# Attention and a rational FFN on one core: units chunk by chunk, four banks of sums, the reciprocal in SBUF

## The chip, the cores and the metric

The kernel runs on one core of one Trainium2 chip. Its time is device microseconds of one execution, the median of three runs. Engines: PE is TensorE (PEld its weight loads), DVE is VectorE, ACT is ScalarE, POOL is GpSimd, SP issues the DMAs. SBUF is the on-chip memory of the engines, PSUM the eight banks (128 x 512 fp32 each) into which PE writes.

## The reference

Two attentions in a row with 32 learned keys (`p`) for each head, and then a feed-forward layer whose activation is a rational function.

```python
def sm_attn(qq, kk, vv):
    s = scale * np.matmul(qq, kk.transpose(0, 1, 3, 2))
    a = np.exp(s - np.max(s, axis=-1, keepdims=True))
    a = a / (np.sum(a, axis=-1, keepdims=True) + 1e-09)
    return np.matmul(a, vv)
p_packed = sm_attn(p, k, v)              # 8 batches, 8 heads, 576 tokens, 64 wide
x = sm_attn(q, p_packed, p_packed)       # to (4608, 512)
h = x @ w_in                             # 512 x 2048
P = a[0] + a[1] * h + a[2] * h**2 + a[3] * h**3
Q = 1.0 + np.abs(b[0]) * np.abs(h) + np.abs(b[1]) * h**2
out = (P / (Q + 1e-6)) @ w_out           # 2048 x 512
```

The weights w_in and w_out come as float64; the kernel gets their 64-bit words.

## The kernel before

**Work and units.** There are 8 batches of 576 tokens. A batch's tokens are cut in two halves (x = 0, 1) of 288, and the 2048 columns between the two weight matrices in 8 chunks (c) of 256. One half of a batch with one chunk is a *unit*: 128 units in all, 16 for each batch (`units`, line 888). The second attention's product with w_in is folded: `m_chunk` (line 786) multiplies the packed values by one or two chunks of w_in into m, and `hidden` (line 814) multiplies m by the attention weights AH (and their low parts AL).

**A unit** goes through `hidden` in three steps. PE makes two tiles h (two banks in PSUM). ScalarE reads each three times (Y, U, sq), and VectorE makes the numerator Y from Y and h: a TENSOR_TENSOR and a SCALAR_TENSOR_TENSOR for each half; these four are called the front instructions here. GpSimd adds U and sq. Then ScalarE takes V = exp(-ln(U + 1)), and VectorE does three instructions with V, called the V instructions here: Y<-Y,abS,V, then V<-U,V, then Y<-V,Y (one Newton step of the reciprocal). V has a single buffer, in two banks of PSUM (`V_ring`, line 332). At the end Y is divided into a high and a low fp32r part: ScalarE casts gh, GpSimd subtracts gl, and GpSimd copies the last 32 of the half's columns to G.

**Sums.** `acc_block` (line 893) adds a unit's product with w_out to two banks of PSUM, three units later (LAG): three fp32r products (high x high, high x low, low x high) for each of two halves and two banks. The first 12 units (PLAIN) use one fp32 sum instead, with the undivided g and w_out (shown in the trace as two records each); their w_out is divided by `divide` (line 411) at units 11 to 21. Units run half by half, so two banks of sums are enough (`acc_ring`, line 330). `remainder` (line 865) handles the last 64 tokens of every batch, kept in G, for two batches at a time.

**Weights.** `load_words` (line 378) brings the 64-bit words of 16 chunks (8 of w_in, 8 of w_out) into free buffers (m, w), and `convert` (line 429) makes fp32 of them: two ScalarE passes of 1024 columns, and three VectorE instructions: a mask of the sign (TENSOR_SCALAR), a shift-and-or (SCALAR_TENSOR_TENSOR), an integer add of 1024 words (shown as CUSTOM_DVE_ANT_0 in the trace, as ISA in the order).

**Order.** All instructions are recorded and put in order by a `Planner` (line 25): it lists them by a table of costs, ways from engine to engine and DMA times, forward and back for four rounds, and writes each engine's instructions out in the planned order. Loads of the first batch stand first, in the order written (`pin`, line 212). Attention of batch b + 1 runs beside batch b's units, in 16 steps. Where the plan has PE idle in the first 150 us, `idle` (line 992) puts in products with a zero matrix. Nearly every instruction is issued in line 226, so rows are told apart by their tiles.

Of the kernel before, what the change touches and what calls it, by code (L numbers as in the profile page):

```python
# [31 lines left out]
class Planner:  # L32
# [7 lines left out]
    COST = {"vector": (70, 1.04), "scalar": (93, 0.83), "gpsimd": (215, 2.11), "tensor": (15, 0.417)}  # L40
    TRANSPOSE, F32 = (15, 0.834), (30, 1.667)
    WAY = {("vector", "vector"): 127, ("scalar", "scalar"): 143, ("tensor", "tensor"): 0, ("gpsimd", "gpsimd"): 0}
    WAY.update({(f"sync", x): 0 for x in ENGINES})
    PASS = 200
    ROUNDS = 4
    DMA_ISSUE, DMA_DELAY = 600, 2300
# [29 lines left out]
    def cost(self, engine, name, args, kwargs):  # L76
# [7 lines left out]
        if engine == "scalar":  # L84
            fixed += (aps[-1].space == PSUM) * -42 + ("accum_out" in kwargs) * 186 + ("bias" in kwargs) * 93
# [18 lines left out]
    def price(self, engine, calls):  # L104
        if engine != "tensor":
            return sum(self.cost(engine, *x) for x in calls)

        parts = {}
        for name, args, kwargs in calls:
            part = args[1].offset // args[1].ap[0][0], args[0].offset // args[0].ap[0][0]  # L110
            parts[part] = parts.get(part, 0) + self.cost(engine, name, args, kwargs)
        return max(parts.values()) + 7 * (len(calls) - 1)
# [36 lines left out]
    def schedule(self, before, after, rank, back=None):  # L149
# [6 lines left out]
        free = dict.fromkeys(self.ENGINES, 0.0)  # L156
# [3 lines left out]
        now = dma = 0.0  # L160
        left = n
        while left:
            for e in self.ENGINES:
                while soon[e] and soon[e][0][0] <= now:
                    heapq.heappush(ready[e], heapq.heappop(soon[e])[1:])
                if free[e] > now or not ready[e]:
                    continue
                _, i = heapq.heappop(ready[e])
                left -= 1
                start[i] = now  # L170
                end[i] = free[e] = now + self.costs[i]
                if e == "sync":
                    dma = max(dma, end[i]) + self.transfers[i]
                    end[i] = dma + self.DMA_DELAY
                for j in after[i]:
                    need[j] -= 1
                    f = self.ops[j][0]
                    way = self.WAY.get((e, f) if back is None else (f, e), self.PASS)
# [10 lines left out]
    def order(self):  # L189
        n = len(self.ops)  # L190
        self.costs = [self.price(*x) for x in self.ops]
        self.transfers = [self.transfer(calls[0][1]) if engine == "sync" else 0 for engine, calls in self.ops]
        before = self.edges()
# [6 lines left out]
        for r in range(self.ROUNDS):  # L200
# [4 lines left out]
            m = max(end)  # L205
# [52 lines left out]
def attention_rational_ffn(  # L258
# [31 lines left out]
    PLAIN = 12  # L290
    UNDIVIDED = {0: (0, 1), 4: (4, 5), 5: (6, 7)}
    DIVIDE = dict(zip((11, 12, 14, 15, 17, 18, 20, 21), (4, 5, 6, 7, 0, 1, 2, 3)))
    DIVIDED = {4: 1, 5: 2, 6: 3, 7: 4, 0: 5, 1: (2, 3), 2: 0, 3: (0, 4)}
    PRE = 4
    AHEAD = 5
    SCALE = 1.0 / float(D) ** 0.5
# [10 lines left out]
    zero = sb.tile([P, D], F32R, name="zero")  # L307
    win = sb.tile([P, NCH, NCC, CF], F32, name="win")
    G = sb.tile([P, NFC, 2 * REM], F32, name="G")
    cuts = [0, 2 * P, 4 * P, 4 * P + 3 * 2 * NB, 4 * P + 3 * 2 * NB + 30]  # L310
    small = sb.tile([P, cuts[-1]], F32, name="small")

    w_ring = Ring(sb, "w", NCH - 2, [P, 2, 2, DM], F32R)

    half_ring = Ring(sb, "half", 5, [P, 2, DM])
# [20 lines left out]
    def constants():  # L336
        nc.vector.tensor_scalar(zero, ident[:, 0:D], 0.0, None, ALU.mult)
# [30 lines left out]
    due = lambda x: x[1] // 2 + (LAG if x[0] == "out" else -2)  # L368
# [3 lines left out]
    room = [((m_ring, i), index["in", 4 * i] + 1) for i in range(NCH // 2)]  # L372
    room += [((w_ring, i), len(words)) for i in (1, 2, 3)]
    room += [((w_ring, i), index["out", 2 * UNDIVIDED[i][0]]) for i in (4, 5)]
    started = False
    words_in, converted = [], 0

    def load_words(n):
        while len(words_in) < min(len(words), converted + n):
            r = len(words_in)  # L380
            kind, i, n2 = words[r]
            used = [x for x, _ in words_in]
            free = [x for x, end in room if r < end and x not in used[converted:]]
            free = [x for x in free if x[0] is not w_ring or x[1] not in (2, 3) or started]
            if not free:
                return
            x = min(free, key=lambda x: max((j for j in range(r) if used[j] == x), default=-1))
            raw = x[0].at(x[1], [P, n2 * 512], I64)
# [8 lines left out]
            words_in.append((x, raw))  # L397

    W, X = {}, {}

    def undivided(c):
        if c not in X:
            pair = [i for i in UNDIVIDED if c in UNDIVIDED[i]]
            if pair:
                t = w_ring.at(pair[0], dtype=F32)
                X.update({y: t[:, x] for x, y in enumerate(UNDIVIDED[pair[0]])})
            else:
                X[c] = half_ring.at(c - 2)
        return X[c]

    def divide(c):
        place = DIVIDED[c]
        if isinstance(place, int):
            t = w_ring.at(place)
            hi, lo = W[c] = t[:, 0], t[:, 1]
        else:
            hi, lo = W[c] = [half_ring.at(i, dtype=F32R) for i in place]
        nc.scalar.copy(hi, X[c])
        for f in range(2):
            nc.gpsimd.tensor_sub(lo[:, f], X[c][:, f], hi[:, f].bitcast(F32))  # L420

    def o_next(dtype=None):
        return half_ring.at(1 if 3 in W else 4, dtype=dtype)
# [5 lines left out]
    def convert():  # L429
# [4 lines left out]
        (kind, i, n), raw = words[converted], words_in[converted][1]  # L434
# [4 lines left out]
        if kind == "in":  # L439
            dst = win[:, i // 2]  # L440
            di = dst.bitcast(I32)
        else:
            dst = undivided(i // 2)
# [597 lines left out]
```

## Time and profile before

| | us |
|---|---|
| median of 3 runs (786.75 to 788.15) | 787.98 |
| span of the profiled execution, first to last instruction | 786.0 |
| TensorE clock granted, mean | 0.987 |
| waits of ScalarE's sq on PE's h, in total | 31.0 |
| waits of VectorE's Y on ScalarE's V, in total | 23.0 |
| waits of PE on the first DMA of K | 15.2 |

The profile's page gives each engine's busy time, its busy share in 40 slices, the chain of work that ended last, and groups of equal instructions. A group's row has the line, the engine, the operation, the tiles written and read (buffer numbers left out), the shape, the count, then the busy time in us and the mean of one in ns, then the engine's idle time just before and what ended it. A row of the timeline has the start and the length in us, the engine, the operation and, in brackets, the idle time before it. A row of the chain has start, length and what it was. A busy PE is not necessarily PE at its peak.

### The profile page before, as it was taken

The numbers are of one execution on the slowest core, as the hardware profiler recorded it, in microseconds if no ns is written. First come the engines' busy times: TensorE is split into PE (matmuls) and PEld (weight loads), VectorE is DVE, ScalarE is ACT, GpSimd is POOL, SyncE is SP. The second block draws the span as 40 slices with busy tenths as digits, with TensorE's granted clock in tenths as the row PEclk, the third lists the DMA queues.
The fourth block names the chain that finished last, engine by engine and source line by source line (L and its number), as shares of the span: only waits on it lengthen the run. The fifth ranks groups of instructions, "written<-read, shape, count | busy, mean of one in ns | idle before, by whom it ended". The sixth has DMA issues, their size and how long they took to land.

```text
span 786.0 us, 14945 instructions
## 1 busy us (share of the span) xinstructions
PE 745.8 (95%) x5336; PEld 567.5 (72%) x5336; DVE 693.2 (88%) x1295; ACT 657.8 (84%) x1464; POOL 453.6 (58%) x448
## 2 busy tenths in 40 slices
PE   2679999999999999999999999999999999999997
PEld 1345555588778887678778887678787887778886
DVE  4899999998999789998999789998999789988873
ACT  5869978988896998888897898889798788998872
POOL 0012448757585665756686555756587556766663
PEclk9959999999999999999999999999999999999999
DMA  9984353023601155023601136023701132000001
GB/s 297 332 296 143 108 100 49 1 85 46 110 1 55 45 66 90 1 85 46 95 17 55 44 52 104 1 58 62 94 28 54 41 45 46 1 22 7 27 1 41
DMA packets 152027, 56.03 MB, mean 71 GB/s; under 512 B 122256, under 2 KB 141200, under 8 KB 151952
## 3 DMA queue, kind: packets, MB, share of 16 engines
q1 hardware_dynamic: 151952, 55.07, 30.7%
q8 instruction: 42, 0.69, 0.4%
q14 instruction: 33, 0.27, 0.1%
HBM read 45.62 MB, written 9.44 MB: 70 GB/s over the span
## 4 chain that ended last, share of the span: by engine, by line
PE 76%; ACT 10%; DVE 8%; DMA 4%; issue 1%; POOL 0%; SPq 0%; DVEq 0%; ACTq 0%
PE acc L226 38%; PE h L226 24%; PE at L226 14%; DVE Y L226 4%; ACT Y L226 2%; DMA nat<-in_k_dram 2%; DVE w L226 2%; ACT V L226 1%; ACT U L226 1%; ACT sq L226 1%; ACT kx L226 1%; ACT w L226 1%; DMA m<-in_moe_w_in_dram 1%; ACT m L226 1%; DVE small L226 1%
## 5 line engine op out<-in xcount | busy, mean ns | idle before, releaser
L226 POOL TENSOR_TENSOR U<-U,sq 128x576 f32<-128x576 f32 x128 | 184.1, 1438 | 109.1 <-ACT U L226 55.8
L226 PE MATMUL acc<-w,gh 128*128 128x512 f32 x736 | 239.3, 408 | 1.6 <-ACT gh L226 1.4
L226 PE MATMUL h<-AH,m 128*128 128x288 f32 x1024 | 201.1, 320 | 7.9 <-DVE Y L226 5.6
L226 PEld LDWEIGHTS h<-AH,m 128*128 128x128 f32 x1024 | 163.0, 191 | 45.8 <-DVE Y L226 22.6
L226 POOL TENSOR_TENSOR gl<-Y,gh 128x512 fp32r<-128x512 f32 x116 | 150.2, 1295 | 39.0 <-issue 14.3
L226 PEld LDWEIGHTS acc<-w,gh 128*128 128x128 f32 x736 | 131.8, 188 | 45.5 <-issue 11.8
L226 PE MATMUL acc<-w,gl 128*128 128x512 f32 x384 | 147.9, 412 | 0.0
L226 ACT ACTIVATE Y<-h,abS 128x288 f32<-128x288 f32 x256 | 126.3, 511 | 23.2 <-PE h L226 19.7
L226 ACT ACTIVATE sq<-h 128x288 f32<-128x288 f32 x256 | 107.0, 419 | 39.2 <-PE h L226 31.0
L226 DVE TENSOR_TENSOR Y<-Y,h 128x288 f32<-128x288 f32 x256 | 109.1, 444 | 26.3 <-ACT Y L226 9.7
L226 DVE SCALAR_TENSOR_TENSOR Y<-Y,abS,h 128x288 f32<-128x288 f32 x256 | 124.5, 504 | 2.2
L226 DVE SCALAR_TENSOR_TENSOR Y<-Y,abS,V 128x576 f32<-128x576 f32 x128 | 102.8, 803 | 23.6 <-ACT V L226 23.0
L226 ACT ACTIVATE U<-h 128x288 f32<-128x288 f32 x256 | 98.6, 424 | 9.8 <-PE h L226 4.7
L226 ACT ACTIVATE V<-U,one 128x576 f32<-128x576 f32 x128 | 98.4, 769 | 5.6 <-DVE Y L226 3.8
L226 PE MATMUL h<-AL,m 128*128 128x288 f32 x448 | 96.1, 295 | 0.0
L226 DVE SCALAR_TENSOR_TENSOR V<-U,V 128x576 f32<-128x576 f32 x128 | 96.0, 750 | 0.0
L226 PEld LDWEIGHTS acc<-w,gl 128*128 128x128 f32 x384 | 71.9, 188 | 23.9 <-issue 9.6
L226 DVE SCALAR_TENSOR_TENSOR Y<-V,Y 128x576 f32<-128x576 f32 x116 | 86.7, 748 | 1.9
L226 POOL COPY G<-Y 128x64 f32<-128x64 f32 x116 | 27.5, 237 | 102.6 <-DVE Y L226 95.6
L226 ACT ACTIVATE V<-V 128x576 f32<-128x576 f32 x128 | 84.8, 663 | 0.7
L226 PE MATMUL acc<-half,gh 128*128 128x512 f32 x240 | 78.4, 413 | 1.3 <-ACT gh L226 0.9
L226 ACT CAST gh<-Y 128x512 fp32r<-128x512 f32 x116 | 73.4, 632 | 6.0 <-DVE Y L226 5.5
(135 smaller groups left out, 984.1 us busy)
## 6 DMA issues: line engine op xcount, KB each, us to landing
w<-in_moe_w_out_dram SPq DMA_DIRECT2D x16, 512.0 KB, 4.6
out_dram<-half SPq DMA_DIRECT2D x15, 512.0 KB, 3.1
nat<-in_k_dram SPq DMA_DIRECT2D x48, 144.0 KB, 3.9
nat<-in_q_dram SPq DMA_DIRECT2D x48, 144.0 KB, 4.3
nat<-in_v_dram SPq DMA_DIRECT2D x24, 256.0 KB, 3.7
m<-in_moe_w_in_dram SPq DMA_DIRECT2D x8, 512.0 KB, 6.2
w<-in_moe_w_in_dram SPq DMA_DIRECT2D x8, 512.0 KB, 8.2
nat<-in_k_dram SPq DMA_DIRECT2D x4, 512.0 KB, 7.7
```

Of the source, the lines that this page charges most:

```text
L226: getattr(getattr(self.nc, engine), name)(*args, **kwargs)
```

## The change

- `units` runs chunk by chunk, both halves in turn; `acc_ring` has four banks, and `V_ring` is in SBUF, so that PSUM holds four banks of sums, two of h and two of the rest.
- PLAIN, `undivided` and `divide` are gone. A w_out chunk is divided as it is converted (ScalarE casts the high part, GpSimd subtracts the low one in two instructions), and every unit uses three fp32r products.
- The sign mask of `convert` is a GpSimd TENSOR_SCALAR in place of the VectorE one.
- Buffers for the words and for whole w_out chunks are two lists (RAW, WHOLE); chunks are due at twice the distance.
- The first loads are in another order, m_chunk, remainder and conversions stand at other units, and the transposed last keys go into kx by two copies in place of one into small.
- The planner has other costs and ways, a start time for each engine, a rule for GpSimd and some VectorE instructions that share a port (`shares`: TENSOR_SCALAR, copies and the integer add on SBUF alone), a limit of DMAs in flight, slack in the backward pass and eight rounds.

```diff
-    COST = {"vector": (70, 1.04), "scalar": (93, 0.83), "gpsimd": (215, 2.11), "tensor": (15, 0.417)}
+    COST = {"vector": (70, 1.04), "scalar": (93, 0.83), "gpsimd": (150, 2.14), "tensor": (15, 0.418)}
...
+    def shares(self, engine, calls):
+
+        if engine == "gpsimd":
+            return True
+        if engine != "vector":
+            return False
+        name, args, _ = calls[0]
+        aps = [x for x in args if isinstance(x, bass.AP)]
+        if any(x.space == PSUM for x in aps):
+            return False
+        return name in ("tensor_scalar", "tensor_copy") or (name == "tensor_add" and aps[0].dtype == I32)
...
-    PLAIN = 12
-    UNDIVIDED = {0: (0, 1), 4: (4, 5), 5: (6, 7)}
...
+    RAW = "m0 m1 m2 m3 w1 w2 w3 w4 m2 m3 w6 w7 w5 m0 m3 m0".split()
+    WHOLE = "o0 w5 o0 o0 m1 w6 o0 m1".split()
...
-    acc_ring = Ring(ps, "acc", 2, [P, DM])
+    V_ring = Ring(sb, "V", 1, [P, 2, HALF])
+    acc_ring = Ring(ps, "acc", 4, [P, DM])
     h_ring = Ring(ps, "h", 2, [P, 512])
-    V_ring = Ring(ps, "V", 1, [P, 2, 512])
     at_ring = Ring(ps, "at", 2, [P, 512])
...
-    due = lambda x: x[1] // 2 + (LAG if x[0] == "out" else -2)
+    due = lambda x: x[1] + (LAG if x[0] == "out" else -2)
...
-        nc.vector.tensor_scalar(lo, hi, -0x80000000, None, ALU.bitwise_and)
+        nc.gpsimd.tensor_scalar(lo, hi.bitcast(F32), 0.0, -2.0**31, ALU.is_lt, ALU.mult)
         nc.vector.scalar_tensor_tensor(hi, hi, 3, lo, ALU.logical_shift_left, ALU.bitwise_or)
-        nc.vector.tensor_add(dst.bitcast(I32), hi, di)
+        nc.vector.tensor_add(di, hi, di)
+        if kind == "out":
+            t = w_ring.at(i // 2)
+            wh, wl = W[i // 2] = t[:, 0], t[:, 1]
+            nc.scalar.copy(wh, dst)
+            for f in range(2):
+                nc.gpsimd.tensor_sub(wl[:, f], dst[:, f], wh[:, f].bitcast(F32))
...
-    units = [(bb, x, c) for bb in range(B) for x in range(2) for c in range(NCH)]
+    units = [(bb, x, c) for bb in range(B) for c in range(NCH) for x in range(2)]
...
-        if u < PLAIN:
-            for f in range(2):
-                g = GS[bb, x, c][:, f, cols]
-                nc.tensor.matmul(acc, g, X[c][:, f, :], start=c == 0 and f == 0, stop=c == NCH - 1 and f == 1)
...
-    for what in (2, "r", 3, "p", "k0", "k1", "qr", 4, "rv", "v0", "v1", 5, "q0", "q1"):
+    for what in ("r", "p", "qr", "k0", "k1", 1, "rv", "v0", "v1", 2, "q0", "q1", 3, 4):
```

How it moves instructions is shown at three places. First the DMA issues of SP at the program's start, before (AH is the buffer of the last keys there, pn of p, nat of K, m, w of words or of V and Q):

```order
L226 DMA m_1_75<-in_moe_w_in_dram 128x2x256 x2
L226 DMA m_2_76<-in_moe_w_in_dram 128x2x256 x2
L226 DMA AH_1_77<-in_k_dram 64x8x64
L226 DMA m_3_78<-in_moe_w_in_dram 128x2x256 x2
L226 DMA pn_1_79<-in_p_dram 32x2x64 x4
L226 DMA nat_1_80<-in_k_dram 128x4x256
L226 DMA nat_2_81<-in_k_dram 128x4x256
```

And the same place of SP after the change:

```order
L288 DMA AH_1_75<-in_k_dram 64x8x64
L288 DMA pn_1_76<-in_p_dram 32x2x64 x4
L288 DMA AH_1_75<-in_q_dram 32x4x128 x2
L288 DMA nat_1_77<-in_k_dram 128x4x256
L288 DMA nat_2_78<-in_k_dram 128x4x256
L288 DMA m_1_79<-in_moe_w_in_dram 128x2x256 x2
```

K (nat) is now ahead of all words of the weights; three loads of words stood ahead of it.

Second GpSimd from the first unit on, before (U is the denominator, half and w are w_out):

```order
L226 TENSOR_TENSOR U0_1_125<-U0_1_125,sq0_1_128 128x576
L226 TENSOR_TENSOR U1_2_137<-U1_2_137,sq0_2_140 128x576
L226 TENSOR_TENSOR U0_3_151<-U0_3_151,sq0_3_154 128x576
L226 TENSOR_TENSOR U1_4_166<-U1_4_166,sq0_4_169 128x576
L226 COPY pn0_3_241<-pn0_3_241 128x2x64
L226 TENSOR_TENSOR U0_5_180<-U0_5_180,sq0_5_183 128x576
L226 TENSOR_TENSOR half3_6_350<-w0_10_161,half2_5_349 128x512 x2
```

GpSimd at the same place after the change (TENSOR_SCALAR of 1024 columns is the mask):

```order
L288 TENSOR_TENSOR U0_1_127<-U0_1_127,sq0_1_130 128x576
L288 TENSOR_SCALAR w4_6_120<-w4_6_120 128x1024
L288 TENSOR_TENSOR w1_9_143<-w5_8_142,w1_9_143 128x512
L288 TENSOR_TENSOR U1_2_134<-U1_2_134,sq0_2_137 128x576
L288 COPY G_73<-Y0_1_129 128x2x32
L288 TENSOR_TENSOR w1_9_143<-w5_8_142,w1_9_143 128x512
L288 TENSOR_TENSOR gl0_1_160<-Y0_1_129,gh0_1_159 128x512
L288 TENSOR_TENSOR U0_3_150<-U0_3_150,sq0_3_153 128x576
```

Between two U of successive units there now stand masks, low parts of w_out, copies to G and gl.

Third PE at the first unit's sums (acc0 and acc1 are its two banks), before:

```order
L226 MATMUL acc0_13_171<-w0_10_161,gh0_1_160 128x512 x2
L226 MATMUL h0_7_170<-AH0_3_113,m1_6_134 128x288 x2
L226 MATMUL h1_8_175<-AH0_3_113,m1_6_134 128x288 x2
L226 MATMUL at1_28_178<-win_72,ppT0_1_88 32x256
L226 MATMUL at0_29_179<-win_72,ppT0_1_88 32x256
```

PE at that place after the change:

```order
L288 MATMUL acc0_13_169<-w0_7_122,gh0_1_159 128x512 x2
L288 MATMUL acc1_14_170<-w0_7_122,gh0_1_159 128x512 x2
L285 MATMUL acc1_14_170<-w0_7_122,zero_71 32x256 x2
L288 MATMUL h0_7_168<-AH0_3_112,m0_6_124 128x288 x2
L288 MATMUL acc0_13_169<-w0_7_122,gl0_1_160 128x512
L288 MATMUL acc0_13_169<-w0_7_122,gh0_1_159 128x512 x2
L288 MATMUL acc1_14_170<-w0_7_122,gl0_1_160 128x512
L288 MATMUL acc1_14_170<-w0_7_122,gh0_1_159 128x512 x2
```

The two fp32 sums of a bank became six products, with gl among them, so that PE's sums now need GpSimd's gl; zero products stand where the plan has PE idle (12 in the first program, 55 now).

More of the change, by code (lines that the diff above doesn't have):

```diff
@@ L84, in cost @@
         if engine == "scalar":
-            fixed += (aps[-1].space == PSUM) * -42 + ("accum_out" in kwargs) * 186 + ("bias" in kwargs) * 93
+            fixed += (aps[-1].space == PSUM) * -42 + ("accum_out" in kwargs) * 93 + ("bias" in kwargs) * 93
+            per += 0.1 * any(x.ap[-1][0] == 2 for x in aps[:2])
+        if engine == "gpsimd" and len(aps) < 3:
+            fixed, per = 135, 0.9
         if engine == "vector" and len(aps) > 2 and any(self.columns(x) == 1 for x in aps[1:]):
@@ L147, in edges, with schedule @@
         return edges
-    def schedule(self, before, after, rank, back=None):
+    def schedule(self, before, after, rank, back=False):
         n = len(rank)
@@ L381, in load_words @@
             kind, i, n2 = words[r]
[L382 to L385, printed above, removed]
+            if RAW[r] in RAW[converted:r]:
                 return
-            x = min(free, key=lambda x: max((j for j in range(r) if used[j] == x), default=-1))
-            raw = x[0].at(x[1], [P, n2 * 512], I64)
+            raw = place(RAW[r], [P, n2 * 512], I64)
             if kind == "in":
@@ L396, in load_words @@
                     nc.sync.dma_start(raw[:, 512 * y : 512 * (y + 1)], w_out[(i + y) * P : (i + y + 1) * P, :])
[L397 to L418, printed above, removed]
-        for f in range(2):
-            nc.gpsimd.tensor_sub(lo[:, f], X[c][:, f], hi[:, f].bitcast(F32))
-    def o_next(dtype=None):
-        return half_ring.at(1 if 3 in W else 4, dtype=dtype)
+            words_in.append(raw)
+    W = {}
     def split(x, hi, lo, eng=nc.gpsimd):
@@ L676, in attention @@
                     nc.tensor.transpose(t[0:REM, o], KX[:, i, NS * P : T], ident)
-                nc.scalar.copy(eTr, t[:, 0 : NG * P])
+                for i in range(2):
+                    to = KX[rows(i), 2 : 2 + NG, NS * P : T]
+                    nc.scalar.copy(to, t[rows(i), 0 : NG * P].rearrange("p (r c) -> p r c", r=NG)[:, :, rows(i)])
             yield
@@ L909, in acc_block @@
         if i == 0:
-            O[bb, x] = o_next()
+            O[bb, x] = o_ring.next()
         o = O[bb, x]
```

136 lines of the change are left out of this document (81 added, 55 removed).

## The prediction

> **What bounds the kernel now.** I read the page's sums first, then the busy time by stretches, then the chain that ended last, then groups by shape, and at the end two places of the timeline. The sums say that TensorE (PE) is the busiest engine and that VectorE (DVE) is not far behind; the stretches say where.
>
> ```profile
> PE 745.8 (95%) x5336; PEld 567.5 (72%) x5336; DVE 693.2 (88%) x1295; ACT 657.8 (84%) x1464; POOL 453.6 (58%) x448
> 50.00:161.00 111.00, 105.98 (x621) 59.47 (x622) 106.21 (x195) 99.35 (x208) 56.74 (x44) 0.95 0.34 95
> 161.00:697.00 536.00, 530.95 (x3992) 422.18 (x3991) 486.47 (x920) 460.58 (x1054) 342.54 (x343) 1.00 0.29 52
> 697.00:773.00 76.00, 75.03 (x393) 63.59 (x392) 62.67 (x110) 62.70 (x143) 49.18 (x50) 1.00 0.04 15
> ```
>
> Columns of the last three rows: stretch, its length, busy PE, PEld, DVE, ACT, POOL, then clock and DMA. Up to 50 us lies the start. From 50 to 161 us the first batch's 16 units go through VectorE: PE and VectorE are both busy for 106 of 111 us. From 161 to 697 us run six batches, 5.58 us a unit (536 over 96), PE 99% busy: PE is the bound. The last batch has no attention beside it: 76 us, 4.75 us a unit, PE again. So a gain must come from the start or the first batch, or from PE's own work; a loss can come wherever VectorE, with 50 idle us in 536 (0.52 a unit), gets more to do.
>
> **The change part by part.**
>
> *Start.* The order shows three loads of w_in words (two DMAs of 512 KB each) moved behind K.
>
> ```profile
> GB/s 297 332 296 143 108 100 49 1 85 46 110 1 55 45 66 90 1 85 46 95 17 55 44 52 104 1 58 62 94 28 54 41 45 46 1 22 7 27 1 41
> m<-in_moe_w_in_dram SPq DMA_DIRECT2D x8, 512.0 KB, 6.2
> 9.95 5.10 DMA nat<-in_k_dram
> 50.50 0.44 DVE L226 TENSOR_TENSOR Y<-Y,h 128x288 f32<-128x288 f32 x1
> ```
>
> K lands at 15.05 us. With 3 MB fewer ahead of it, at 297 GB/s, it lands up to 10 us sooner, but 1.4 MB and the first issue stay ahead: about 7 us, so 8 sooner. The first unit reaches VectorE at 50.50 us; I let it come 8 us earlier (between 0, if the words become the last wait, and 9).
>
> *PE's sums.* 48 fp32 sums (12 units, two banks, two halves) become 144 fp32r products.
>
> ```profile
> 122.14 2.77 PE acc L226 x6
> 240.28 1.36 PE acc L226 x6
> ```
>
> In the chain, six fp32 records are three sums: 0.92 us each, 44 in all. Six fp32r records are six products: 0.23 each, 33 in all. PE's work falls by about 11 us. That counts only where PE is the bound in the first batch.
>
> *VectorE and GpSimd share something.* These rows decide the case:
>
> ```profile
> L226 DVE SCALAR_TENSOR_TENSOR m<-m 128x1024 int32<-128x1024 int32 x4 | 4.9, 1226 | 0.1
> 59.21 1.42 POOL L226 TENSOR_TENSOR U<-U,sq 128x576 f32<-128x576 f32 x1 [7.35 <-ACT sq L226]
> 60.10 1.62 DVE L226 SCALAR_TENSOR_TENSOR w<-w 128x1024 int32<-128x1024 int32 x1
> 24.20 0.16 DVE L226 SCALAR_TENSOR_TENSOR small<-small 128x2 f32<-128x2 f32 x1
> 349.95 1.30 POOL L226 TENSOR_TENSOR gl<-Y,gh 128x512 fp32r<-128x512 f32 x1 [0.69 <-POOL U L226]
> 350.42 0.84 DVE L226 SCALAR_TENSOR_TENSOR small<-small 128x2 f32<-128x2 f32 x1
> ```
>
> A VectorE instruction with both inputs in SBUF takes 1.226 us alone and 1.62 when a GpSimd one is running: it ends 1.09 us after GpSimd's end (60.63). A two-column one, 0.16 us alone, takes 0.84 and ends 0.01 us after GpSimd's end. So each waits for the GpSimd instruction to end, and only its first 0.14 us lie beside it. One input in PSUM makes the difference. Here is a unit of the last batch, where V is in PSUM:
>
> ```profile
> 711.65 0.82 DVE L226 TENSOR_TENSOR Y<-Y,h 128x288 f32<-128x288 f32 x2 [0.17 <-ACT U L226]
> 712.38 0.93 DVE L226 SCALAR_TENSOR_TENSOR Y<-Y,abS,h 128x288 f32<-128x288 f32 x2
> 713.59 0.81 DVE L226 SCALAR_TENSOR_TENSOR Y<-Y,abS,V 128x576 f32<-128x576 f32 x1 [0.28 <-ACT V L226]
> 714.33 0.76 DVE L226 SCALAR_TENSOR_TENSOR V<-U,V 128x576 f32<-128x576 f32 x1
> 715.12 0.76 DVE L226 SCALAR_TENSOR_TENSOR Y<-V,Y 128x576 f32<-128x576 f32 x1
> 716.04 0.45 DVE L226 TENSOR_TENSOR Y<-Y,h 128x288 f32<-128x288 f32 x1 [0.17 <-ACT U L226]
> 711.99 1.43 POOL L226 TENSOR_TENSOR U<-U,sq 128x576 f32<-128x576 f32 x1 [0.20 <-ACT U L226]
> 713.38 1.29 POOL L226 TENSOR_TENSOR gl<-Y,gh 128x512 fp32r<-128x512 f32 x1
> ```
>
> GpSimd's gl runs from 713.38 to 714.67, and VectorE's first V instruction starts inside it and still takes its 0.81. The change puts V into SBUF: all three V instructions of all 128 units then have two SBUF inputs and cannot run beside GpSimd. In this unit the first would end at about 714.67 + 0.81 - 0.14 = 715.34, not 714.40: 0.94 late. Behind it on VectorE stand the other two and the next unit's four front instructions. V has one buffer, so ScalarE's next Ln waits for the third: the delay goes around the loop from unit to unit.
>
> The Trainium skill, "SBUF — State Buffer", section "Who interferes with whom", states this as a rule: a DVE instruction with two SBUF inputs contends with a GpSimd instruction that reads SBUF, whichever is first holds the pair for the whole instruction, and one with at most one SBUF input is free of it. The rows above agree (0.84 against 0.16, and 0.81 unharmed). By the rule for all V instructions the sum below stands; without it the first rival's.
>
> *First batch.* Between VectorE's first Y instruction and its last of unit 15 the new order has, with two SBUF inputs, 48 V instructions, 10 shift-and-or of 1024 columns and 12 integer adds; GpSimd has 16 U, 13 gl, 14 G, 13 lows of w_out, 9 masks, 4 kx, 2 AL and a copy.
>
> ```profile
> L226 DVE SCALAR_TENSOR_TENSOR Y<-Y,abS,V 128x576 f32<-128x576 f32 x128 | 102.8, 803 | 23.6 <-ACT V L226 23.0
> L226 DVE SCALAR_TENSOR_TENSOR V<-U,V 128x576 f32<-128x576 f32 x128 | 96.0, 750 | 0.0
> L226 DVE SCALAR_TENSOR_TENSOR Y<-V,Y 128x576 f32<-128x576 f32 x116 | 86.7, 748 | 1.9
> L226 DVE CUSTOM_DVE_ANT_0 win<-m,win 128x2048 uint16<-128x2048 uint16 x4 | 4.9, 1223 | 0.1
> L226 POOL TENSOR_TENSOR U<-U,sq 128x576 f32<-128x576 f32 x128 | 184.1, 1438 | 109.1 <-ACT U L226 55.8 <-ACT sq L226 40.5 <-DVE Y L226 7.6
> L226 POOL TENSOR_TENSOR gl<-Y,gh 128x512 fp32r<-128x512 f32 x116 | 150.2, 1295 | 39.0 <-issue 14.3 <-ACT gh L226 12.0 <-POOL G L226 6.3
> L226 POOL COPY G<-Y 128x64 f32<-128x64 f32 x116 | 27.5, 237 | 102.6 <-DVE Y L226 95.6 <-DVE small L226 6.1 <-ACT sq L226 0.5
> L226 POOL TENSOR_TENSOR w<-half,w 128x512 fp32r<-128x512 f32 x2 | 2.6, 1280 | 2.0 <-ACT w L226 2.0
> 1.01 0.29 POOL masks.py:199 TENSOR_SCALAR_AFFINE_SELECT ident<-ident 128x128 f32<-128x128 f32 x1
> L226 POOL TENSOR_TENSOR kx<-kx,small 128x576 f32<-128x576 f32 x28 | 32.6, 1163 | 8.6 <-DVE small L226 8.5
> L226 POOL TENSOR_TENSOR AL<-kx,AH 128x576 fp32r<-128x576 f32 x14 | 20.0, 1436 | 0.2
> L226 DVE TENSOR_SCALAR w<-w 128x1024 int32<-128x1024 int32 x12 | 9.7, 808 | 1.4 <-ACT win L226 1.4
> ```
>
> VectorE: 16 x 2.301 = 36.8, 10 x 1.226 = 12.3, 12 x 1.223 = 14.7: 63.8 us. GpSimd: 23.0 + 16.8 + 3.3 + 16.6 + 4.7 + 2.9 + 0.3 = 67.6, and the masks. A mask of 1024 columns is in no row: from 64 columns (0.237) to 128 (0.29) one input costs 0.83 ns a column, so 1.03 us; at two inputs' rate it would be twice 1.295. I take 1.03, nearest in kind: 9.3 (up to 23). Together 140.7 us that exclude each other, less 0.14 us for each change of hands, at most 140 of them: 121. Between 121 and 141 I take 131 for a stretch of 111 now: +20. VectorE's other work lies beside GpSimd's 77 us. Taking the masks off VectorE saves 0.81 each there, inside this sum. PE's 106 us, 11 less, are then no bound, so its saving is hidden, as are ScalarE's 12 new casts and lows.
>
> *Six batches.* As in the unit shown, one GpSimd instruction falls on the V instructions of each unit, about 0.94 us late; the loop of 4.39 us (711.65 to 716.04) becomes 5.33, under PE's 5.58. But in these batches VectorE also has attention: 486.47 / 96 = 5.07 busy a unit. If its waits come on top, a unit takes 5.07 + 0.94 + some idle, up to 6.18; if its attention work hides GpSimd's, 5.58. Between 0 and 0.6 a unit I take the half: 0.3 x 96 = 29 us. *Last batch:* 5.33 instead of 4.75 would be 9; half its idle 13 us may take it: 5.
>
> Four banks and the new unit order take away waits of PE:
>
> ```profile
> PE h L226 <- DVE Y L226: 5.6, 11, 1.9
> ```
>
> These 5.6 us are all there is for h, and VectorE, now later, causes them; I count nothing. The split copy of the last keys and the 55 zero products (12 before) lie in idle time of ScalarE and PE; if not, they cost a few us in the first 150, inside the first batch's bounds.
>
> **Sum** against the profiled execution: 786.0 - 8 + 20 + 29 + 5 = 832; the median of the runs is 787.98, 2.0 above that span: **834 us**.
>
> **Rivals.** (1) *The planned gain*: the V instructions meet GpSimd seldom or go first, and GpSimd, 36% idle in the six batches, takes all the waiting. Then PE stays the bound and the start and the fp32 sums pay: 786 - 8 - 11 + 2 = 769. It decides if VectorE's waits stay under its 0.52 idle us a unit and the first batch under 111. For it: GpSimd has the time. Against: gl at 713.38 is ahead of V by 0.21 us, and 121 is over 111. (2) *Hidden in the six batches*, paid in the first alone: 786 - 8 + 20 + 2 = 800. (3) *All waits on VectorE*: 141 in the first batch (+30), 0.6 a unit (58), 9 at the end: 786 - 8 + 30 + 58 + 9 + 2 = 877. (4) The change does nothing, its start and its waits in balance: 788.
>
> **How the numbers follow.** Forecast 0.50, rival 1 0.13, rival 2 0.20, rival 3 0.15, rival 4 0.02. The range goes from rival 4's side, 786, to 880, past rival 3; rival 1 and a few per cent above are left out. Faster by over 0.2% is rival 1, 0.13; within 0.2%, about what a measurement can tell from no change, 0.02; slower 0.85.
>
> **What would show it.** The means of the three V groups rise from 0.80, 0.75 and 0.75 us towards 1.1 or more, and GpSimd's U and gl above 1.44 and 1.30, with overlaps gone; VectorE's busy share rises over 95% while PE's falls below 92%; the first batch's stretch on VectorE is 120 us or longer, from a beginning near 42 us; PE waits on VectorE far longer than 5.6 us. Means of V unchanged beside busy GpSimd would prove the sharing wrong, and the time would then be near 769.

## The result, and the profile after

The changed kernel takes 939.0 us (median of 4 runs, 937.8 to 941.4), the kernel before 787.5 (786.8 to 788.2): a ratio of 1.193, 95% interval 1.191 to 1.196. It is slower, by 151 us where 46 were forecast, and beyond the 880 us at which the range ended.

Of the page after: the sums, then the busy time in the stretches that answer to those shown of before (the second column is the length, then busy PE, PEld, DVE, ACT, POOL, clock and DMA).

```profile
PE 792.9 (85%) x5415; PEld 591.3 (63%) x5415; DVE 840.4 (90%) x1267; ACT 679.1 (73%) x1484; POOL 606.0 (65%) x488
50.00:203.00 153.00, 118.49 (x742) 78.60 (x741) 135.88 (x181) 107.39 (x221) 139.46 (x81) 0.89 0.26 72
203.00:832.00 629.00, 558.49 (x3966) 424.09 (x3965) 596.29 (x916) 470.02 (x1059) 385.29 (x340) 0.98 0.25 44
832.00:923.00 91.00, 81.13 (x415) 65.69 (x414) 79.65 (x114) 67.59 (x146) 52.42 (x50) 0.98 0.03 12
```

In the six middle batches VectorE is now busy for 596 of 629 us (95%) and PE for 89%: VectorE has become the bound, and PE waits for it. In the first batch GpSimd is the fullest engine, 139 of 153 us. VectorE does a few instructions fewer than before and is busy 147 us longer. The groups say which:

```profile
L288 DVE SCALAR_TENSOR_TENSOR Y<-Y,abS,V 128x576 f32<-128x576 f32 x128 | 154.1, 1204 | 21.3 <-ACT V L288 20.4
L288 DVE SCALAR_TENSOR_TENSOR V<-U,V 128x576 f32<-128x576 f32 x128 | 153.7, 1201 | 3.3
L288 DVE SCALAR_TENSOR_TENSOR Y<-V,Y 128x576 f32<-128x576 f32 x128 | 123.4, 964 | 1.6
L288 POOL TENSOR_TENSOR U<-U,sq 128x576 f32<-128x576 f32 x128 | 205.3, 1604 | 88.7 <-ACT U L288 42.6
L288 POOL TENSOR_SCALAR m<-m 128x1024 int32<-128x1024 f32 x9 | 35.5, 3946 | 22.2 <-ACT win L288 17.9 <-DVE o L288 3.0 <-ACT o L288 1.3
L288 POOL TENSOR_SCALAR w<-w 128x1024 int32<-128x1024 f32 x7 | 28.0, 4023 | 4.0 <-ACT o L288 3.5 <-DMA pn<-in_p_dram 0.6
```

The three V groups took 803, 750 and 748 ns before; a unit's three take 1.07 us more now, 137 us over 128 units. The sixteen masks take 3.95 and 4.02 us each, 63.5 us of GpSimd in all. Among the waits (total us, times, longest), PE's on VectorE for a free h went from 5.6 to 73.4 us, and VectorE now waits for masks:

```profile
PE h L288 <- DVE Y L288: 73.4, 70, 3.5
DVE m L288 <- POOL m L288: 11.3, 5, 3.7
```

The time between the ends of V<-U,V of the 16th, 112th and 128th unit cuts every run into the same four stages (us; the last one to the end of the span):

| kernel | first batch, from 0 | six batches | last batch | tail | span |
|---|---|---|---|---|---|
| before | 160.3 | 536.2 | 76.2 | 13.2 | 786.0 |
| after | 203.0 | 629.4 | 90.5 | 13.2 | 936.0 |
| difference | +42.6 | +93.1 | +14.3 | 0 | +150.0 |
| forecast (start and first batch, six, last) | +12 | +29 | +5 | 0 | +46 |

All three stages lost more than forecast, the six batches most.

### The profile page after: what moved, and what is told of

It is laid out like the page before. It is cut to its first block, busy times and chain, and to the rows that moved or that the text cites. A ratio compares the mean times of both kernels' runs of the same rounds, so it can differ in the third digit from the quotient of the medians.

```text
span 936.0 us, 15228 instructions
## 1 busy us (share of the span) xinstructions
PE 792.9 (85%) x5415; PEld 591.3 (63%) x5415; DVE 840.4 (90%) x1267; ACT 679.1 (73%) x1484; POOL 606.0 (65%) x488
## 4 chain that ended last, share of the span: by engine, by line
DVE 56%; ACT 17%; PE 6%; issue 4%; POOL 2%; DMA 1%; DVEq 0%; POOLq 0%; SPq 0%; ACTq 0%
DVE Y L288 32%; DVE V L288 13%; ACT V L288 8%; DVE small L288 4%; DVE kx L288 3%; DVE m L288 3%; PE acc L288 2%; ACT gh L288 2%; PE h L288 2%; ACT U L288 2%; ACT Y L288 2%; ACT sq L288 1%; ACT kx L288 1%; PE at L288 1%; POOL gl L288 1%
## 5 line engine op out<-in xcount | busy, mean ns | idle before, releaser
L288 PE MATMUL acc<-w,gh 128*128 128x512 f32 x1024 | 330.8, 407 | 5.2 <-ACT gh L288 4.3
L288 PE MATMUL h<-AH,m 128*128 128x288 f32 x1024 | 212.1, 330 | 79.0 <-DVE Y L288 73.4
L288 POOL TENSOR_TENSOR U<-U,sq 128x576 f32<-128x576 f32 x128 | 205.3, 1604 | 88.7 <-ACT U L288 42.6
L288 PEld LDWEIGHTS acc<-w,gh 128*128 128x128 f32 x1024 | 192.7, 194 | 53.1 <-issue 10.5
L288 POOL TENSOR_TENSOR gl<-Y,gh 128x512 fp32r<-128x512 f32 x128 | 187.0, 1461 | 54.5 <-ACT gh L288 36.3
L288 PE MATMUL acc<-w,gl 128*128 128x512 f32 x512 | 195.9, 408 | 12.9 <-POOL gl L288 12.7
L288 DVE SCALAR_TENSOR_TENSOR Y<-Y,abS,V 128x576 f32<-128x576 f32 x128 | 154.1, 1204 | 21.3 <-ACT V L288 20.4
L288 ACT ACTIVATE Y<-h,abS 128x288 f32<-128x288 f32 x256 | 126.7, 509 | 46.5 <-POOL gl L288 27.8
L288 DVE SCALAR_TENSOR_TENSOR V<-U,V 128x576 f32<-128x576 f32 x128 | 153.7, 1201 | 3.3
L288 DVE SCALAR_TENSOR_TENSOR Y<-V,Y 128x576 f32<-128x576 f32 x128 | 123.4, 964 | 1.6
L288 PEld LDWEIGHTS acc<-w,gl 128*128 128x128 f32 x512 | 97.6, 192 | 39.1 <-POOL gl L288 19.6
L288 PEld LDWEIGHTS h<-AL,m 128*128 128x128 f32 x448 | 73.5, 192 | 0.1
```

The costliest lines, as they stand in the source:

```text
L288: getattr(getattr(self.nc, engine), name)(*args, **kwargs)
```

## The experiments

### One part undone, or one part alone

**a1**: the changed kernel with the mask back on VectorE.

```diff
-        nc.gpsimd.tensor_scalar(lo, hi.bitcast(F32), 0.0, -2.0**31, ALU.is_lt, ALU.mult)
+        nc.vector.tensor_scalar(lo, hi, -0x80000000, None, ALU.bitwise_and)
```

> The changed kernel with the sign mask back on VectorE (bitwise_and), nothing else. Theory L (V in SBUF makes VectorE and GpSimd exclude each other) leaves the six middle batches at 6.55 us a unit, and takes from the first batch 16 GpSimd instructions of 3.95 us for 16 VectorE ones of 0.8: about 20 to 30 us less, 910 to 920 us. Theory M (the masks, 64 us of GpSimd, are the loss): more than 60 us less, 875 us or below. If the masks were hidden: 939.

908.3 us (ratio to before 1.152 to 1.156): 31 less. Its first batch ends at 185.7, 17 us sooner, and its six batches still take 615.9. So the masks are about a fifth of the loss. The first Y instruction on VectorE is at 44.14 us, against 53.03 after and 50.50 before.

**b1**: the kernel before with V in SBUF (and the smaller zero matrix and the two copies of the last keys that make room for it).

```diff
...
-    V_ring = Ring(ps, "V", 1, [P, 2, 512])
+    V_ring = Ring(sb, "V", 1, [P, 2, HALF])
...
-        U, V, Y = U_ring.next(), V_ring.next()[:, :, 0:HALF], Y_ring.next()
+        U, V, Y = U_ring.next(), V_ring.next(), Y_ring.next()
...
```

> The kernel before with V in SBUF in place of two PSUM banks; to make room for it the last keys are copied into kx by two copies and the zero matrix has 32 columns, as in the change. Theory L: the three V groups go from 803, 750, 748 ns to over 1100 and the six middle batches from 5.58 to over 6 us a unit: 840 to 900 us. Theory P (the new order of units and the new planner are the loss): 788 plus or minus 5, and the groups stay within 0.1 us unless the planned order keeps them apart.

881.6 us (1.117 to 1.123): this part alone costs 94 us. The groups are at 1229, 992 and 856 ns; over 1100 was expected of all three. By stage: 178.9, 599.7, 87.7, that is +18.5, +63.4 and +11.5. TensorE's granted clock is 0.984 here (0.987 before, 0.956 after), so this loss does not come from the clock.

**b2**: the kernel before with the mask on GpSimd (the edit of a1 turned around). **b3**: the kernel before with the whole class `Planner` of the change.

> The kernel before with the sign mask on GpSimd, nothing else. GpSimd's share of the first batch was 57 of 111 us; 16 masks of 3.95 us are 63 more, some 12 of them there. Theory L leaves V free in PSUM, so the loss is what the masks delay of U: 5 to 25 us, 793 to 813 us. Theory M: 830 us or more.

> The kernel before with the changed planner (costs, ways, start times, port rule, slack, eight rounds), nothing else; its port rule knows no scalar_tensor_tensor. Theory L: the planner is no part of the loss, 775 to 800 us. Theory P: 830 us or more.

b2 took 797.0 us (1.011 to 1.015), 10 more, all of it in the first batch (171.3). b3 took 781.5 us (0.991 to 0.995): the new planner with the old program is the fastest kernel of this study. The planner by itself is no part of the loss.

### Do the parts add, can an order avoid the waits, and what does a mask cost?

**b4** is b1 and b3 together. **a3** is a1 with the planner's port rule rewritten:

```diff
-        aps = [x for x in args if isinstance(x, bass.AP)]
-        if any(x.space == PSUM for x in aps):
-            return False
-        return name in ("tensor_scalar", "tensor_copy") or (name == "tensor_add" and aps[0].dtype == I32)
+        ins = [x for x in args[1:] if isinstance(x, bass.AP) and x.space != PSUM and self.columns(x) > 1]
+        return len(ins) > 1
```

> The kernel before with V in SBUF and the changed planner together, old order of units, masks on VectorE. Alone, V in SBUF gave 881.6 and the planner 781.5 against 787.3. If they add, 876 plus or minus 5. If the changed planner, which counts U, gl and the copies as holding a port and the V instructions as not, makes the meetings of V and GpSimd worse, 890 to 910, and it accounts for most of what a1 (908.3) has over V alone; if not, the unit order and the undivided first units account for it.

> The mask on VectorE as in a1 (908.3), and the planner's port rule told of the pair as the trace shows it: a VectorE instruction holds it when it has two inputs in SBUF of more than one column, and no other does. GpSimd's work and the V instructions together are 3.6 + 2.3 us of a unit's 6.4, so an order exists in which they hardly wait. If the waits are the order's fault: 820 to 880 us, the three V groups nearer 750 ns. If the exclusion itself sets the time (VectorE, GpSimd and ScalarE bound by it in a loop): 900 to 915.

b4: 890.6 us (1.129 to 1.133). With the new planner V in SBUF costs 109, 15 more than with the old one; its port rule does not name the V instructions. a3: 869.8 us (1.101 to 1.106), 38 less than a1 by nothing but the order. Count a V instruction as held up when it takes over 0.1 us more than the mean of its group before. In the six batches of a1 GpSimd's U then held up a V instruction 34 times, in a3 once; gl held one up 73 times, then 82. The waits of the first V instruction on gl stay (1288 ns); the second and third recover in part:

```profile
L286 DVE SCALAR_TENSOR_TENSOR Y<-Y,abS,V 128x576 f32<-128x576 f32 x128 | 164.9, 1288 | 22.4 <-ACT V L286 21.5
L286 DVE SCALAR_TENSOR_TENSOR V<-U,V 128x576 f32<-128x576 f32 x128 | 122.1, 954 | 1.8
L286 DVE SCALAR_TENSOR_TENSOR Y<-V,Y 128x576 f32<-128x576 f32 x128 | 109.4, 854 | 2.1
```

**c1** is b3 with the first loads in the order K, then words:

```diff
-    for what in (2, "r", 3, "p", "k0", "k1", "qr", 4, "rv", "v0", "v1", 5, "q0", "q1"):
+    for what in ("r", "p", "qr", "k0", "k1", 1, "rv", "v0", "v1", 2, "q0", "q1", 3, 4, 5):
```

> The kernel before with the changed planner and K ahead of the words, nothing else: V in PSUM, masks on VectorE, old units. In a1 the first h ran at 34.4 us, in the kernel before at 43.3. If that start is kept through the first batch, 781.5 - 8 = 773 us; if the words, now later, hold up the units behind, 781 or more.

786.2 us (0.9976 to 0.9995): the start is not kept. The first Y comes at 44.10 us, 6.4 sooner than in the kernel before and 4.8 sooner than in b3, and the first batch yet ends at 162.3, later than b3's 156.6. No single wait took it: VectorE is full from there on. From the first Y to the end of the batch it idles 3.1 of 118.2 us (1.2 of 107.6 in b3). Up to that end it is busy for 143.0 us in c1 and 142.0 in b3; c1 does 27.8 of them ahead of the first Y, b3 35.6. So 7.8 us of VectorE's work only moved behind the first Y, and it idled 3.0 us more ahead of it.

**p1** puts eight GpSimd forms on a scratch tile, twice, ahead of the kernel before:

```diff
...
+    for _ in range(2):
+        nc.gpsimd.tensor_scalar(x2i[:, :, 0], s2[:, :, 1], 0.0, -2.0**31, ALU.is_lt, ALU.mult)
+        nc.gpsimd.tensor_scalar(si[:, 0:1024], hi, 0.0, -2.0**31, ALU.is_lt, ALU.mult)
+        nc.gpsimd.tensor_scalar(lo, hi, 0.0, 2.0, ALU.is_lt, ALU.mult)
+        nc.gpsimd.tensor_scalar(lo, hi, 2.0, None, ALU.mult)
+        nc.gpsimd.tensor_scalar(s2[:, :, 0], s2[:, :, 1], 2.0, None, ALU.mult)
+        nc.gpsimd.tensor_scalar(lo[:, 0:256], hi[:, 0:256], 0.0, 2.0, ALU.is_lt, ALU.mult)
+        nc.gpsimd.tensor_copy(lo, hi)
+        nc.gpsimd.tensor_sub(lo, lo, hi)
```

> The kernel before with 16 GpSimd instructions on a scratch tile ahead of its work (and one VectorE fill), two rounds of eight forms of 1024 columns: is_lt and mult from fp32 at every second word to int32 at every second word (the mask); the same contiguous; the same to fp32; mult alone, contiguous and at every second word; is_lt and mult on 256 columns; a copy; a subtraction. Its own time means nothing. If the mask's 3.9 us come from the second operation, mult alone takes about half; if from the stride, the contiguous forms do; if from the int32 output, the fp32 one; if it is the plain rate of a TENSOR_SCALAR there, all take 3.9 and 256 columns about 1.0, and a copy 0.9 and a subtraction 2.5.

Each form in the first round, as a stretch around it (length, then GpSimd's busy time; the order is that of the code):

```profile
3.07:6.78 3.71, 3.71 (x1) 1.00 1.04 402
6.86:10.49 3.63, 3.63 (x1) 1.00 1.08 297
10.58:15.18 4.60, 4.60 (x1) 1.00 1.10 341
15.26:18.30 3.04, 3.04 (x1) 1.00 1.08 307
18.38:21.28 2.90, 2.89 (x1) 1.00 1.12 307
21.47:22.55 1.08, 1.08 (x1) 1.00 1.11 355
22.61:23.65 1.04, 1.04 (x1) 1.00 1.06 381
23.73:26.09 2.36, 2.35 (x1) 1.00 1.06 377
```

Neither the stride (3.71 against 3.63) nor the int32 output (3.63, with fp32 4.60) makes a mask dear, and a single operation is not half of it (3.04 and 2.89; 3.69 and 3.38 in the second round). Every TENSOR_SCALAR of 1024 columns took 2.9 to 4.6 us. From 256 to 1024 columns it grows by 3.4 ns a column against the first form ((3.71 - 1.08) / 768) and by 4.6 against its own (4.60). A copy of the same size takes 1.04. The fourth answer is nearest: it is the rate of this instruction there. How the forms differ among each other is less sure: VectorE stood idle beside the first (3.71), the 256 columns and the copy, and converted weights beside the next four.

### Is it GpSimd's work, or V's place?

**a2** is a1 without gl, **b7** the kernel before without gl:

```diff
-        gh, gl = GS[bb, x, c] = gh_ring.next(), gl_ring.next()
-        split(Y[:, :, 0:HMAIN], gh, gl)
+        gh = gh_ring.next()
+        GS[bb, x, c] = gh, gh
+        nc.scalar.copy(gh, Y[:, :, 0:HMAIN])
```

> The mask on VectorE as in a1 (908.3), and GpSimd's subtraction gl left out: PE's third product reads gh in its place, so PE, ScalarE and VectorE do the same number of instructions and the low part of g is missing from the result. GpSimd loses 177 of its 600 us. Theory L: every V instruction that came upon a gl waited for its end; in the trace after, gl stands ahead in some 65 of 120 such meetings, with 0.6 to 0.9 us each: 50 to 70 us less, 840 to 860. If GpSimd's share does not matter to VectorE: 900 to 908.

> The kernel before with gl left out in the same way (the low part of g missing from the result); V is in PSUM. Theory L: the same 150 us of GpSimd's work gone are worth nothing here, 783 to 788. If the work of GpSimd delays VectorE or PE in another way, as much as in the run without gl in the changed kernel: 740 or less.

b7: 783.7 us (0.9945 to 0.9973), 3 less: with V in PSUM, 146 us of GpSimd's work are worth next to nothing. a2: 881.5 us (1.118 to 1.121), 27 less than a1, about half of what was expected, with a third of GpSimd's work gone (532 us in a1, 356 here). With gl gone the planner put U ahead of the second V instruction instead: V<-U,V is now at 1242 ns (1041 in a1), Y<-Y,abS,V at 965 (1279). In the six batches U held up 71 V instructions in place of 34, and all of GpSimd's work 101 in place of 144. Most of the meetings moved; they did not go.

**b6** is b4 with a3's port rule, **b5** is b3 with it.

> The old order of units with V in SBUF and the changed planner (890.6), its port rule now told of the pair. In the new order of units the same rule took 908.3 to 869.8. If the waits that are left are the V instructions' own, this comes to 850 to 865 and stays 60 or more above 781.5; what the run a3 then has over it is the new order with its undivided first units gone.

> The kernel before with V in PSUM, the changed planner (781.5) and the same corrected port rule. Only attention's and conversion's VectorE instructions have two inputs in SBUF here. If meetings in attention cost anything, 772 to 780; else 780 to 784.

b6: 882.2 us (1.120 to 1.123), 8 less than b4 where 25 to 40 were expected. So the rule helps the new order of units much more (38) than the old one. In the old order it only traded one kind of meeting for another: in b4's six batches U held up 32 V instructions and gl 57, in b6's U 8 and gl 77, and the total stayed (126 and 129). In the new order the total fell from 144 to 119. b5: 784.1 us (0.996 to 0.998), 2.6 above b3: where V is in PSUM the rule has nothing to gain.

### V back in PSUM within the change

After these runs the share of V inside the changed kernel was still only inferred. **e1** is the changed kernel with V in PSUM; its two banks come from the sums, which the halves share. **e2** has the mask on VectorE as well.

```diff
-    V_ring = Ring(sb, "V", 1, [P, 2, HALF])
-    acc_ring = Ring(ps, "acc", 4, [P, DM])
+    V_ring = Ring(ps, "V", 1, [P, 2, 512])
+    acc_ring = Ring(ps, "acc", 2, [P, DM])
...
-            ACC[bb, x] = [acc_ring.next() for _ in range(2)]
+            ACC[bb] = [acc_ring.next() for _ in range(2)]
...
```

> The changed kernel with V in two banks of PSUM again. The banks come from the sums: both halves of a batch are summed in one pair of banks, and that pair is written for either half, so the result holds the sum of the halves; every engine does as many instructions as in the changed kernel, masks on GpSimd, order chunk by chunk. If V's place is the main loss: 150 less 10 to 40 for the masks remain, 800 to 825. If the order or the planner carries a part of it by itself: 850 or more.

> As the run with V back in PSUM and the halves summed together, and the mask on VectorE too: what is left is the new order, no undivided units, the new planner and K ahead of the words. If these cost nothing: 775 to 785 like the planner alone (781.5) or the planner and K first (786.2). Undivided units gone add 12 gl, 12 G and 12 lows of w_out to GpSimd and 36 us less of PE's sums: 770 at best. Against a1 (908.3) the difference is V's price in the changed order: about 125.

**e3** is a2 with the sum of U and sq left out too:

```diff
-            if f == 1:
-                nc.gpsimd.tensor_add(U, U, U2)
```

> The mask on VectorE, V in SBUF, and neither gl (gh in its place) nor the sum U + sq on GpSimd: the denominator lacks its square and the result its low part. GpSimd keeps G, kx, AL and the lows of w_out. Without gl alone it was 881.5, with U now ahead of the second V instruction. If the loss is the meetings of V with GpSimd's two-input instructions, they are now the few with kx and AL, and the time falls to within 15 us of the run with V in PSUM and the mask on VectorE, the V groups to 780 to 900 ns. If V in SBUF is slow for another reason, 860 or more.

e1: 831.5 us (1.054 to 1.057), 107.5 less than the changed kernel; it falls between the two answers (800 to 825, or 850 and more). e2: 807.5 us (1.024 to 1.027), 101 less than a1 where about 125 were expected, and 22 above the 785 at which its range ended: the rest of the change is not free. The 36 us of PE's sums in that expectation have no row behind them; the prediction's sum was 11. e3: 801.2 us (1.015 to 1.019), V still in SBUF, and 6 us less than e2; its V groups are 853, 854 and 829 ns. The six batches of e1, then of e3:

```profile
191.50:736.00 544.50, 530.04 (x3947) 423.84 (x3946) 483.14 (x915) 456.57 (x1058) 338.62 (x340) 0.99 0.28 51
165.00:706.00 541.00, 528.59 (x3958) 418.14 (x3935) 502.42 (x919) 457.12 (x1052) 90.39 (x148) 1.00 0.29 52
```

VectorE is back to 483 busy us and PE to 97% in the first; in the second GpSimd has 90 us of work in place of 339. Either cure, moving V or taking GpSimd's two-input instructions away, ends most of the loss there: 545 and 542 us for the six batches, against 629. That is the exclusion and nothing else about SBUF: in the six batches of e3 VectorE is busy 502 - 483 = 19 us longer than in e1, and the 31 V instructions still held up there, by kx, AL and the remainder's lows, come to 20 us. One thing is left open: what the sum U + sq costs with V in PSUM was not measured (gl alone was worth 3 us in b7), so e3's time and e2's are not a clean pair; the V groups and the busy times above are what carries this.

e1 and e2 together split the 151 us: V's place 107.5 (939.0 to 831.5), the masks 24 (831.5 to 807.5), and 20 for everything else (807.5 to 787.5). By stage, from the spans (us):

| stage | V's place (after less e1) | masks (e1 less e2) | the rest (e2 less before) |
|---|---|---|---|
| first batch, from 0 | 11.5 | 23.2 | 7.9 |
| six batches | 84.6 | 0.5 | 8.0 |
| last batch | 12.3 | 0.0 | 2.0 |
| tail | -2.5 | 0.0 | 2.5 |

The parts depend a little on each other: with V in SBUF the masks cost 31 (a1), and each run is ordered anew, which alone can move some us (b5 against b3: 2.6). In the 20 of the rest lie the new planner with K first (786.2 in c1, so about -1), the new order of units, the undivided units gone, and the halves' shared banks, which must be copied out before the next batch and are e1's and e2's own. The tail's 2.5 belong to the shared banks, for the changed kernel's tail is as short as before (13.2); whatever else they cost makes V's place dearer by as much. The rest is not separated: with V in PSUM there is no room for four banks of sums, so that was not tried.

## Why the prediction was right or wrong

The mechanism was right, and it is nearly the whole of the loss; the sum failed in its sizes. The largest failed step is the cover: half of the V instructions' delay was to be hidden in the six batches, and nearly all of it came on top (+93 us for +29). The others are the price of a mask (3.9 us for 1.03) and the 8 us credited for the earlier start.

**The exclusion: right.** It holds row by row. Here are two units of the last batch, after, VectorE's rows and then GpSimd's:

```profile
850.88 1.62 DVE L288 SCALAR_TENSOR_TENSOR Y<-Y,abS,V 128x576 f32<-128x576 f32 x1 [0.36 <-ACT V L288]
852.53 0.76 DVE L288 SCALAR_TENSOR_TENSOR V<-U,V 128x576 f32<-128x576 f32 x1
...
856.21 1.94 DVE L288 SCALAR_TENSOR_TENSOR Y<-Y,abS,V 128x576 f32<-128x576 f32 x1 [0.30 <-ACT V L288]
858.19 1.74 DVE L288 SCALAR_TENSOR_TENSOR V<-U,V 128x576 f32<-128x576 f32 x1
859.96 0.76 DVE L288 SCALAR_TENSOR_TENSOR Y<-V,Y 128x576 f32<-128x576 f32 x1
850.57 1.31 POOL L288 TENSOR_TENSOR gl<-Y,gh 128x512 fp32r<-128x512 f32 x1
...
854.86 1.43 POOL L288 TENSOR_TENSOR U<-U,sq 128x576 f32<-128x576 f32 x1 [0.47 <-ACT U L288]
856.24 1.30 POOL L288 TENSOR_TENSOR gl<-Y,gh 128x512 fp32r<-128x512 f32 x1
857.49 1.82 POOL L288 TENSOR_TENSOR o<-G,o 128x512 fp32r<-128x512 f32 x1
```

gl ends at 851.88, and the V instruction, begun at 850.88, ends 0.62 us later, at 852.50: its first 0.14 us lay beside gl, the rest came after. The next V instruction meets nobody and takes 0.76. The next unit shows both sides waiting by turns: Y<-Y,abS,V starts while U still runs (to 856.29), gl gets in ahead of it, and it waits for gl's end too (857.54); the remainder's low o waits for it (1.82 us), V<-U,V waits for o (to 859.31) and takes 1.74. Before, the same first instruction took 0.81 with gl running. In all of the trace 221 V instructions start inside a GpSimd TENSOR_TENSOR. 219 of them end 0.61 to 0.79 us after it (median 0.61); of the two others one is the case just shown, and one got ahead of a gl that was itself waiting for VectorE.

**Six batches: the mechanism right, both factors of its size wrong.** The step was "one GpSimd instruction falls on the V instructions of each unit, about 0.94 us late", of which half was to be hidden. In the trace of the six batches, 149 of the 288 V instructions (96 units, three each) were held up: 1.55 a unit, 0.71 us each, 1.10 us a unit. gl held 74 of them, U 42, kx, AL and the remainder's lows the other 33. So there were more meetings than counted, each shorter, and together only a little more than 0.94. The large miss is the cover. VectorE's busy time rose by 596.3 - 486.5 = 109.8 us, 1.14 a unit; its idle time fell by only 49.5 - 32.7 = 16.8, and the other 93.0, 0.97 a unit, are what the six batches lost, where 0.3 a unit was forecast. VectorE was 91% busy before and gave up a third of its idle time; "half" had no row behind it. Rival 3, all waits on VectorE, was the nearer one, and still too small at 0.6 a unit (58): of the 0.37 that it lacks, 0.20 are waits beyond its 0.94, and 0.17 are idle time that VectorE kept (0.34 a unit, where the rival left 0.17).

**Last batch: the same**, +14.3 for +5, "half its idle 13 us may take it": it didn't. VectorE's idle time there only fell from 13.3 to 11.4 us.

**First batch: the price of a mask was wrong by four.** "One input costs 0.83 ns a column, so 1.03 us" came from rows of a copy and a select, "nearest in kind". They weren't: a mask takes 3.9 us, beyond the upper bound of 2.6 that two inputs' rate gave. (The Trainium skill, "GPSIMD Engine Reference", section "4.1 Engine selection", calls one input roughly line-rate; p1 has that for a copy, 1.04 us, and 2.9 to 4.6 for a TENSOR_SCALAR.) V's part of this stage was not undersized: 18.5 us in b1 and 11.5 between the changed kernel and e1, for +20 forecast for all of the exclusion. The masks came on top, with 23.2 (e1 less e2). GpSimd's groups in the stretch from 50 to 203 us:

```profile
L288 POOL TENSOR_TENSOR U<-U,sq 128x576 f32<-128x576 f32 x17 | 28.8, 1697 | 2.1 <-issue 1.4 <-ACT U L288 0.7
L288 POOL TENSOR_SCALAR m<-m 128x1024 int32<-128x1024 f32 x5 | 20.0, 4000 | 3.0 <-DVE o L288 3.0
L288 POOL TENSOR_SCALAR w<-w 128x1024 int32<-128x1024 f32 x5 | 19.9, 3999 | 3.5 <-ACT o L288 3.5
```

Ten masks fall there, 40 us where 9.3 were counted, and U stands in line behind GpSimd's other work: only 2.1 us of idle time lie ahead of its 17 instructions. The step that counted masks among the work that excludes VectorE was wrong too, in the other direction. GpSimd's mask, and VectorE's three V instructions beside it:

```profile
62.07 3.76 POOL L288 TENSOR_SCALAR w<-w 128x1024 int32<-128x1024 f32 x1 [3.49 <-ACT o L288]
63.38 0.81 DVE L288 SCALAR_TENSOR_TENSOR Y<-Y,abS,V 128x576 f32<-128x576 f32 x1
64.53 0.75 DVE L288 SCALAR_TENSOR_TENSOR V<-U,V 128x576 f32<-128x576 f32 x1
65.57 0.75 DVE L288 SCALAR_TENSOR_TENSOR Y<-V,Y 128x576 f32<-128x576 f32 x1
```

All three start beside the mask and run at full speed. Of the twelve V instructions that started inside a mask, nine took 0.71 to 0.81 us, three 0.98 to 1.23, and none waited for its end. The Trainium skill, "SBUF — State Buffer", section "Who interferes with whom", lets a VectorE instruction with two SBUF inputs contend with any GpSimd instruction that reads SBUF; that holds here for TENSOR_TENSOR and not for this TENSOR_SCALAR. It holds for GpSimd's one-input copies too, which the prediction's sum did count: a copy of G takes 0.24 us alone, and this one, caught by a shift-and-or of VectorE that ran to 103.09 us, took 1.24 and ended 0.10 after it.

```profile
101.95 1.24 POOL L288 COPY G<-Y 128x64 f32<-128x64 f32 x1
```

Why the TENSOR_SCALAR is exempt no run here shows.

**Start: the earlier K is real, the earlier end is not.** PE's first work on K comes at 8.65 us in place of 15.19. "8 sooner" for the first unit was 6.4 in a1 and c1 and 8.8 in e2. In the changed kernel the masks took it back and more, by a wait that I had not priced, at the head of VectorE's queue:

```profile
15.91 3.84 POOL L288 TENSOR_SCALAR m<-m 128x1024 int32<-128x1024 f32 x1 [10.68 <-ACT win L288]
19.79 1.23 DVE L288 SCALAR_TENSOR_TENSOR m<-m 128x1024 int32<-128x1024 int32 x1 [3.72 <-POOL m L288]
20.93 0.15 DVE L288 TENSOR_TENSOR small<-small 128x2 f32<-128x2 f32 x1
```

A conversion waits 3.72 us for its mask, and the attention's small instructions stand behind it. The first Y then came at 53.03, not near 42. The term itself, 8 us off the end, failed even where no mask stands in the way: in c1 and e2 the first batch began early and ended later than in b3 and before, since VectorE, which the prediction's own row has busy for 106 of 111 us there, is full and has as much work to do whenever the first unit comes.

**PE's sums, hidden: not contradicted.** The 11 us were not counted, and in e2, where VectorE is free again, no gain of that size appears.

**Signs named ahead.** The V groups were to reach 1.1 us: two of three did (1.20, 1.20, 0.96). U and gl above 1.44 and 1.30: 1.60 and 1.46. PE below 92%: 85%. VectorE over 95%: no, 94.8% in the six batches and 90% overall. PE's waits on VectorE far above 5.6 us: 73.4. The first batch 120 us or longer: yes; from a beginning near 42 us: no.

## What to carry to other kernels

Moving one operand of a hot VectorE instruction from PSUM to SBUF can make it and GpSimd's two-input instructions wait for each other; count all such meetings of the loop on both engines. Do not hide half of the waiting by guess: here VectorE was 91% busy, and 93.0 of 109.8 us came on top. An engine that is full from the first unit on gives nothing for an earlier first unit (c1). A planner that orders such a program must be told which instructions exclude each other, and the trace tells which: that was worth 38 us in one order of units and 8 in the other, and did not bring the loss back. An operation that no row shows should not be priced from another instruction of the engine: moving the mask to GpSimd made it five times as long.

## What the hardware showed that was not expected

- GpSimd's TENSOR_SCALAR of 1024 columns takes 2.9 to 4.6 us, in each of the two rounds more than the two-input TENSOR_TENSOR of the same size (2.35 us, and 3.20 with VectorE's two-input instructions beside it), and about three to four times a copy (1.04).
- GpSimd's TENSOR_TENSOR held VectorE's V instruction to its end in 220 of 221 cases, and VectorE's two-input instructions hold GpSimd's copies (1.24 us for 0.24); GpSimd's TENSOR_SCALAR and V instructions run side by side (nine of twelve unharmed). Three shift-and-or instructions of 1024 columns took 2.1 to 2.2 us in place of 1.22 beside a mask (b2), without waiting for its end.
- V instructions with V in SBUF that meet nothing take 0.82, 0.75 and 0.76 us by group (medians), with V in PSUM 0.80, 0.75 and 0.76: SBUF itself is no slower to read here.
